# The decayed queries of groups 1 to 9 on VectorE instead of GpSimd, and a reordered last wide step

## The chip, the cores and the metric

The kernel runs on one core of a Trainium2 chip. A core has five engines that run their own instruction queues side by side: TensorE (PE in the profile; its weight loads are PEld), VectorE (DVE), ScalarE (ACT), GpSimd (POOL) and SyncE (SP), which here issues nearly all DMA transfers. SBUF is the working memory, PSUM holds TensorE's results in banks of 128 x 512 fp32. The metric is the device time of one execution in microseconds.

## The reference

Two blocks follow each other. The first is linear attention with a decay `lam` per head, over 4 sequences of 768 positions with 8 heads of 64; the second picks 128 of the 768 positions of each sequence by a gate and sends them through a two-layer expert.

```python
# attention, block of 64 positions, per head
intra = ((qb @ kb.T) * lam ** (i - j) [i >= j]) @ vb
inter = (qb * lam ** (i + 1)) @ kv_state
out   = intra + inter
kv_state = lam ** 64 * kv_state + (kb * lam ** (63 - j)).T @ vb

# mixture of depths, x = out as (4, 768, 512)
scores = x @ w_gate                          # (4, 768)
top    = the 128 positions with the largest score, per sequence
y      = x; y[top] += sigmoid(scores[top]) * (relu(x[top] @ w1) @ w2)
```

## The kernel before

The work runs in 24 groups of 128 positions (6 per sequence), numbered `g`. The order on every engine is the order in which the program is written; semaphores only hold an instruction until its inputs are there or its buffer is free. The main loop is software-pipelined: step `g` finishes group `g` and starts group `g + 1`.

Groups 0 to 8 are "wide" (`WIDE = 9`): their masked scores are taken over the whole 128 positions. Groups from 9 on are "narrow": two blocks of 64. Step 8 is the last wide step, and it prepares group 9, the first narrow one. From step 8 on, the steps also carry pieces of the expert of an earlier sequence.

The names, as the profile prints them:

- `kn`, `qn`, `vn`: keys, queries and values of a group, loaded by SyncE; `w_sb`: one of 16 pieces (256 KB each) of the expert's weights, eight of w1 (line 103) and then eight of w2 (line 108), loaded by SyncE between the groups. In what place of that queue each stands is set by `WEIGHTS_WITH`: so many pieces behind `kn` (or `qn`) of that group.
- `qT`, `kT`: the transposes. TensorE writes them to a PSUM bank (line 238; in the wide steps `Q_BANK` for the queries, printed as `m`), ScalarE copies them to SBUF (line 242).
- `qs`: the queries times their decay `qpow` (lines 250 and 252), read from `qT` and needed by TensorE in `from_states` (line 357). `kd`: the decayed keys (line 222). `decayed`: the state times its decay (line 327). All three are GpSimd's before.
- `su`: the scores in PSUM; `p`: masked scores (VectorE, line 282 wide, 288 narrow); `o`: the output in PSUM, made from `p` and `vn` (line 369 wide, 377 narrow) and from `state` and `qs` (line 357); `x_b`: the output copied to SBUF (ScalarE, line 399); `state`: the next state (VectorE, line 346).
- `xg`, `sc`: the product with `w_gate` and its sum, the gate score of each position (VectorE, line 419); `sc_row`: these scores as a row (TensorE line 439, ScalarE line 442); `table`: the comparison of a group's scores with those of all earlier positions of its sequence (VectorE, line 449, growing from 128 to 768 columns), whose columns TensorE sums (line 464).
- `xs`: the chosen rows, fetched by an indirect DMA of GpSimd (line 519); TensorE transposes them (line 532, the piece `gate`), ScalarE copies them to `xsT`, and eight pieces `hidden(f)` follow (line 569, 8 matmul instructions each in the trace): `hidden(0)` to `hidden(3)` read the first four pieces of w1, `hidden(4)` to `hidden(7)` the other four, in the order in which they are loaded.

`PIECES` says how many expert pieces a narrow step runs at its three places; in step 9 these lie ahead of `row(8)` (line 439), behind it, and at the step's end.

Step 8 ends on VectorE with `next_state(19)`, then the gate score of group 8, and then `compare(7)`. What waits for the comparison and the score is the start of step 9 on TensorE: `column_sums(7)`, `row(8)`, then `from_scores(9)`.

Of the kernel before, what the change touches and what calls it, by code (L numbers as in the profile page):

```python
# [12 lines left out]
ALU = mybir.AluOpType  # L13
# [4 lines left out]
def kernel(  # L18
# [12 lines left out]
    nc = tc.nc  # L31
# [5 lines left out]
    L = 128  # L37
# [5 lines left out]
    NGR = (CAP + 127) // 128  # L43
# [5 lines left out]
    LINE = 256  # L49
    WIDE = 9  # L50
    WEIGHTS_WITH = {
        "kn": {11: 1, 12: 2, 13: 1, 14: 1, 15: 1, 16: 1},
        "qn": {8: 1, 9: 1, 10: 1, 11: 1, 12: 2, 13: 1, 14: 1, 15: 1}, "vn": {},
    }
    STORES_WITH = {
        "kn": {6: (0,), 7: (1,), 8: (2, 3), 9: (4, 5)}, "qn": {},
        "vn": {11: (6,), 12: (7,), 13: (8,), 14: (9, 10), 15: (11,), 20: (12, 13), 21: (14, 15)},
    }
    PIECES = {9: (0, 1, 3), 13: (1, 0, 1), 14: (1, 0, 1), 15: (1, 0, 2), 20: (1, 0, 1), 21: (1, 0, 1),
              22: (1, 0, 1), 23: (1, 0, 0)}  # L60
    TINY = 2.0 ** -125
    BELOW = TINY * (1.0 - 2.0 ** -24)
# [43 lines left out]
    def w2_load(f):  # L106
# [22 lines left out]
        out=lead[:, (NT - 1) * L :], in_=lead[:, (NT - 1) * L :], compare_op=ALU.is_ge,  # L129
# [84 lines left out]
    def wide(g):  # L214
        return g < WIDE
# [29 lines left out]
    def queries_decayed(g):  # L245
        if g >= NG or (wide(g) and g % NT == 0):
            return
        qs = att.tile([128, NHP, L], FP32, name="qs")
        if wide(g):
            nc.gpsimd.tensor_tensor(out=qs[:], in0=qTs[g], in1=qpow[:], op=ALU.mult)  # L250
        else:
            nc.gpsimd.tensor_tensor(  # L252
                out=qs[:].rearrange("p a (c i) -> p a c i", c=2),
                in0=qTs[g].rearrange("p a (c i) -> p a c i", c=2),
                in1=qpow[:, :, :C].unsqueeze(2).broadcast_to([128, NHP, 2, C]), op=ALU.mult,
            )
        qss[g] = qs
# [158 lines left out]
    def gate_scores(g):  # L416
        b, t = divmod(g, NT)
        xg = mod.tile([128, HD], FP32, name="xg")
        nc.vector.tensor_tensor_reduce(  # L419
            out=xg[:], in0=x_bs[b][:, t].rearrange("p a b e -> p (a b e)"), in1=wg_b[:],  # L420
            scale=1.0, scalar=0.0, op0=ALU.mult, op1=ALU.add, accum_out=scs[b][:, t : t + 1],
        )
# [264 lines left out]
    for g in range(-1, NG):  # L687
        loads_to(g + ahead(g))
        if g < 0:
            keys_decayed(0)  # L690
            transposes(0, "kT")
            transposes(0, "qT")
            scores(0)
            transposes(1, "kT")
            masked(0)
        else:
            transposes(g + 1, "qT")
            if NGR and wide(g):
                row(g - 1)
            if g > 0:  # L700
                transposes(g + 1, "kT")
            if g == 1:
                next_state(2)
        if wide(g):
            if g >= 0:
                state_products(g + 1)
            queries_decayed(g + 1)
            if g == 1:
                decay_state(4)
            if NGR and wide(g + 1) and not ends(g - 2):  # L710
                compare(g - 1)
            if g > 0:
                next_state(2 * g + 2)
            if g >= 0:
                from_scores(g)
                outputs(g)
                if g == 0:
                    nc.scalar.copy(
                        out=decay_w[:], in_=qpow[:, :, L - 1 : L].broadcast_to([128, NHP, D])
                    )  # L720
                    keys_decayed(2)
                    decay_state(2)
                if g not in kept:
                    store(g)
            else:
                state_products(0)
                next_state(0)
                query_powers()
                nc.vector.stream_shuffle(wg_b[:], wg_b[:], first)
            if not wide(g + 1):  # L730
                decay_state(2 * g + 3)
            if g == 2:
                slot_casts()
            if g in (3, 4):
                narrow_mask(g - 3)
            if g == 5:
                narrow_powers()
            if g >= 0:
                if wide(g + 1):
                    gate_scores(g)  # L740
                scores(g + 1)
            if NGR and ends(g - 2):
                from_states(g + 1)
                take((g - 2) // NT)
            if NGR and wide(g + 1):
                column_sums(g - 1)
            if g >= 0:
                masked(g + 1)
            if NGR and ends(g - 2):
                two_to_tok((g - 2) // NT)  # L750
                compare(g - 1)
            if NGR and wide(g + 1) and ends(g - 1):
                find((g - 1) // NT)
            keys_decayed(g + 2)
            if not wide(g + 1):
                next_state(2 * g + 3)
                gate_scores(g)
            elif g + 1 in qss or (g + 1) % NT == 0:
                from_states(g + 1)
            if g > 0:  # L760
                decay_state(2 * g + 4)
            if NGR and ends(g - 2):
                get((g - 2) // NT)
            if NGR and not wide(g + 1):
                compare(g - 1)
                for i in range(NGR):
                    pieces.extend(expert(0, i))
            continue
        now = PIECES.get(g, (1, 1, 1))
        from_states(g)  # L770
        settle(g)
        queries_decayed(g + 1)
        if NGR and ends(g - 3) and g - 3 < 2 * NT:
            get((g - 3) // NT)
        state_products(g + 1)
        next_state(2 * g + 2)
        decay_state(2 * g + 3)
        if NGR:
            column_sums(g - 2)
        if g - 4 >= NT and ends(g - 4) and g - 4 < 2 * NT:  # L780
            for i in range(NGR):
                pieces.extend(expert((g - 4) // NT, i))
        products(now[0])
        if NGR:
            if ends(g - 2) and g - 2 >= 2 * NT:
                take((g - 2) // NT)
                get((g - 2) // NT)
            row(g - 1)
        products(now[1])
        from_scores(g)  # L790
        outputs(g)
        if g not in kept:
            store(g)
        scores(g + 1)
        if NGR:
            compare(g - 1)
        next_state(2 * g + 3)
        masked(g + 1)
        gate_scores(g)
        flush(later)  # L800
        keys_decayed(g + 2)
        decay_state(2 * g + 4)
        products(now[2])
        if NGR and ends(g - 1):
            column_sums(g - 1)
            find((g - 1) // NT)
        if NGR and ends(g - 2) and g - 2 < 2 * NT:
            take((g - 2) // NT)
        if g - 3 >= 2 * NT and ends(g - 3):
            for i in range(NGR):  # L810
                pieces.extend(expert((g - 3) // NT, i))
            products(1)
        flush()
# [57 lines left out]
```

## Time and profile before

| | |
|---|---|
| device time, median of 3 runs | 174.32 us (174.17 to 175.76) |
| the profiled execution, its own time | 174.1 us |
| span of its trace (first to last instruction) | 172.3 us |
| TensorE busy | 159.1 us (92%) |
| VectorE busy | 103.6 us (60%) |
| GpSimd busy | 93.5 us (54%) |
| ScalarE busy | 71.0 us (41%) |
| mean granted clock of TensorE | 0.998 |

The profile is of one execution. Its span leaves out 1.8 us ahead of the first and behind the last instruction, and its own time is 0.2 us under the median. Busy shares are averages over stages that have different limits: a wide stage to about 48 us, narrow steps with expert pieces in between to about 145 us, and the last sequence's expert alone. A timeline row gives the start in microseconds from the start of the span, the length, the engine, the line and the operation; in square brackets stands how long the engine was idle before it and what released it.

### The profile page before, as it was taken

What the parts mean: (1) busy time and instruction counts of PE and PEld (TensorE: products, weight loads), DVE (VectorE), ACT (ScalarE), POOL (GpSimd) and SP (SyncE); (2) the same over time, 40 slices, a digit from 0 to 9 for tenths busy, and PEclk for the clock granted to TensorE, in tenths of its full rate; (3) what the DMA queues carried; (4) which work ended last, traced back from release to release, by engine and by line L of the source; (5) the groups of instructions that cost most, each with busy time, mean ns of one, the idle gap of its engine ahead of it and who ended that gap; (6) DMA issues with size and microseconds to landing.
All of it is one profiled execution on the core that took longest, in us unless ns stands there. A gap on an engine that the chain in (4) does not pass through costs nothing.

```text
span 172.3 us, 7863 instructions
## 1 busy us (share of the span) xinstructions
PE 159.1 (92%) x3436; PEld 131.2 (76%) x3436; DVE 103.6 (60%) x233; ACT 71.0 (41%) x191; POOL 93.5 (54%) x100
## 2 busy tenths in 40 slices
PE   7799999999877979999989999999999999989990
PEld 7689788889666969757757999866777988469970
DVE  3987899898678424766545974575575755240011
ACT  2334655544344435533535554632554544013100
POOL 6369965568796315467687636558658600220022
PEclk9999999999999999999999999999999999999999
DMA  5999899999999999999999899997411111011000
GB/s 132 232 248 225 184 246 269 254 244 287 246 237 249 259 274 269 257 316 256 237 215 232 184 216 287 286 253 196 126 65 65 65 65 61 10 50 65 0 30 30
DMA packets 81345, 31.96 MB, mean 186 GB/s; under 512 B 75676, under 2 KB 75676, under 8 KB 81312
## 3 DMA queue, kind: packets, MB, share of 16 engines
q1 hardware_dynamic: 80640, 29.37, 67.6%
q0 software_dynamic: 656, 2.10, 3.9%
q8 instruction: 27, 0.44, 1.0%
q14 instruction: 6, 0.05, 0.1%
q10 hardware_dynamic: 16, 0.01, 0.0%
HBM read 24.13 MB, written 7.34 MB: 183 GB/s over the span
## 4 chain that ended last, share of the span: by engine, by line
PE 68%; DVE 10%; DMA 6%; issue 6%; POOL 3%; SPq 2%; ACT 2%; POOLq 1%; DVEq 0%; ACTq 0%
PE m L569 16%; PE m L581 13%; PE m L238 8%; PE o L357 6%; PE o L377 5%; PE su L314 5%; PE su L272 4%; DMA w_sb<-in_moe_w_dram 3%; PE o L369 2%; DVE xg L419 2%; PE m L606 2%; DVE p L282 2%; DMA lam_b<-in_lam_dram 2%; DVE mask_w L174 2%; PE m L305 1%
## 5 line engine op out<-in xcount | busy, mean ns | idle before, releaser
L569 PE MATMUL m<-xsT,w_sb 128*128 128x128 f32 x256 | 33.9, 282 | 1.8 <-DMA w_sb<-in_moe_w_dram 1.2
L449 DVE SCALAR_TENSOR_TENSOR table<-sc_row,sc,lead 128x128 bf16<-128x128 f32 (+5 forms) x24 | 26.3, 1097 | 12.9 <-ACT sc_row L442 12.8
L569 PEld LDWEIGHTS m<-xsT,w_sb 128*128 128x128 f32 x256 | 30.5, 192 | 2.9 <-DMA w_sb<-in_moe_w_dram 1.4
L252 POOL TENSOR_TENSOR qs<-qT,qpow 128x512 f32<-128x512 f32 x15 | 20.4, 1362 | 18.1 <-ACT qT L242 16.9
L419 DVE CUSTOM_DVE_ANT_0 xg<-x_b,wg_b 128x512 f32<-128x512 f32 x24 | 24.2, 1009 | 3.1 <-ACT x_b L399 2.5
L327 POOL TENSOR_TENSOR decayed<-state,decay 128x256 f32<-128x256 f32 x25 | 18.9, 756 | 11.7 <-DVE state L346 10.8
L581 PE MATMUL m<-w_sb,hs 128*128 128x512 f32 x48 | 25.0, 623 | 0.0
L242 ACT COPY qT<-m 128x512 f32<-128x512 f32 x24 | 14.1, 587 | 20.4 <-PE m L238 18.2
L346 DVE TENSOR_TENSOR state<-su,decayed 128x256 f32<-128x256 f32 x25 | 10.6, 422 | 18.0 <-PE su L314 9.4
L573 ACT ACTIVATE hs<-m 128x128 f32<-128x128 f32 x32 | 8.9, 278 | 24.3 <-PE m L569 24.3
L222 POOL TENSOR_TENSOR kd<-kn,kpow 128x512 f32<-128x512 f32 x15 | 16.5, 1100 | 0.0
L242 ACT COPY kT<-m 128x512 f32<-128x512 f32 x24 | 14.3, 594 | 3.3 <-PE m L238 3.2
L357 PE MATMUL o<-state,qs 64*64 64x64 f32 x672 | 15.3, 224 | 0.0
L238 PE MATMUL m<-ident,qn 128*128 128x128 f32 x96 | 15.0, 279 | 0.0
L238 PE MATMUL m<-ident,kn 128*128 128x128 f32 x96 | 14.5, 273 | 0.0
L357 PEld LDWEIGHTS o<-state,qs 64*64 64x64 f32 x672 | 12.3, 134 | 2.7 <-issue 2.2
L250 POOL TENSOR_TENSOR qs<-qT,qpow 128x512 f32<-128x512 f32 x7 | 9.7, 1384 | 7.6 <-ACT qT L242 5.9
L222 POOL TENSOR_TENSOR kd<-kn,kpow_w 128x512 f32<-128x512 f32 x9 | 11.9, 1328 | 3.5 <-DVE kpow_w L179 3.5
L377 PEld LDWEIGHTS o<-vn,p 64*64 64x64 f32 x480 | 8.7, 134 | 5.7 <-issue 2.8
L288 DVE TENSOR_TENSOR p<-su,mask 128x512 f32<-128x512 f32 x15 | 10.2, 683 | 4.0 <-PE su L272 4.0
L238 PEld LDWEIGHTS m<-ident,qn 128*128 128x128 f32 x96 | 10.7, 141 | 2.1 <-issue 1.6
L272 PE MATMUL su<-qT,kT 64*64 64x64 f32 x480 | 10.7, 220 | 1.0 <-issue 0.9
(87 smaller groups left out, 249.0 us busy)
## 6 DMA issues: line engine op xcount, KB each, us to landing
kn<-in_k_dram SPq DMA_DIRECT2D x24, 256.0 KB, 4.9
qn<-in_q_dram SPq DMA_DIRECT2D x24, 256.0 KB, 4.6
vn<-in_v_dram SPq DMA_DIRECT2D x24, 256.0 KB, 4.9
out_dram<-x_b SPq DMA_DIRECT2D x24, 256.0 KB, 3.5
w_sb<-in_moe_w_dram SPq DMA_DIRECT2D x16, 256.0 KB, 5.4
xs<-out_dram,tok POOLq DMA_INDIRECT x4, 4.2
out_dram<-y,tok POOLq DMA_INDIRECT x3, 2.9
out_dram<-y_half,half_at POOLq DMA_INDIRECT x2, 2.4
```

The costliest lines, as they stand in the source:

```text
L222: nc.gpsimd.tensor_tensor(out=kd[:], in0=loaded[g][0][:], in1=pw[:].rearrange("p a b -> p (a b)").unsqueeze(2).broadcast_to([128, H, D]), ...
L238: nc.tensor.transpose(tp[:, hp * L : (hp + 1) * L], in_=t[:, 2 * hp : 2 * hp + 2, :], identity=ident[:])
L242: nc.scalar.copy(out=dst[:].rearrange("p a i -> p (a i)"), in_=tp[:])
L252: nc.gpsimd.tensor_tensor(out=qs[:].rearrange("p a (c i) -> p a c i", c=2), in0=qTs[g].rearrange("p a (c i) -> p a c i", c=2), in1=qpow[:, ...
L272: nc.tensor.matmul(su[half[c], hh, hp * C : (hp + 1) * C], lhsT=kT[half[hh], hp, half[c]], rhs=qT[half[hh], hp, half[c]], start=True, stop ...
L327: nc.gpsimd.tensor_tensor(out=t[:], in0=states[n][:], in1=(decay_w if wide(g) else decay)[:], op=ALU.mult)
L357: nc.tensor.matmul(o_[half[c if wide(g) else hh ^ c], hh, hp * D : (hp + 1) * D], lhsT=qs[half[hh], hp, half[c]], rhs=states[n][half[hh], ...
L377: nc.tensor.matmul(o_[half[hh ^ c], hh, hp * D : (hp + 1) * D], lhsT=p[half[c], hh, hp * C : (hp + 1) * C], rhs=vn[half[c], 2 * hp + hh, : ...
L419: nc.vector.tensor_tensor_reduce(out=xg[:], in0=x_bs[b][:, t].rearrange("p a b e -> p (a b e)"), in1=wg_b[:], scale=1.0, scalar=0.0, op0=A ...
L449: nc.vector.scalar_tensor_tensor(out=table[:, : (t + 1) * L], in0=rows_[b][:, : (t + 1) * L], scalar=scs[b][:, t : t + 1], in1=lead[:, (NT ...
L569: nc.tensor.matmul(ph, lhsT=w1_sb[:, dc, f * 128 : (f + 1) * 128], rhs=keep["xsT"][:, dc, :], start=(dc == 0), stop=(dc == NDC - 1),)
L581: nc.tensor.matmul(py[:], lhsT=keep["hs"][:, f, :], rhs=w2_sb[:, f, :], start=(f == 0), stop=(f == NFC - 1),)
```

## The change

Four edits. Line numbers of the changed kernel are five higher from `queries_decayed` on.

1. `queries_decayed` for groups 1 to 5, 7 and 8 (wide; groups 0 and 6 start a sequence and have none) and for group 9 is issued to VectorE and reads the transposes from `Q_BANK` in PSUM instead of their copy `qT` in SBUF. The 14 later groups stay on GpSimd as before. The copy by ScalarE stays; scores still read it.
2. In step 8, `compare(7)` stands ahead of `gate_scores(8)`.
3. `PIECES[9]`: the expert's `gate` piece of step 9 stands ahead of `row(8)` instead of behind it.
4. `WEIGHTS_WITH`: `kn` of group 11 is followed by two weight pieces instead of one, `qn` of group 12 by one instead of two.

```diff
     WEIGHTS_WITH = {
-        "kn": {11: 1, 12: 2, 13: 1, 14: 1, 15: 1, 16: 1},
-        "qn": {8: 1, 9: 1, 10: 1, 11: 1, 12: 2, 13: 1, 14: 1, 15: 1}, "vn": {},
+        "kn": {11: 2, 12: 2, 13: 1, 14: 1, 15: 1, 16: 1},
+        "qn": {g: 1 for g in range(8, 16)}, "vn": {},
     }
...
-    PIECES = {9: (0, 1, 3), 13: (1, 0, 1), 14: (1, 0, 1), 15: (1, 0, 2), 20: (1, 0, 1), 21: (1, 0, 1),
+    PIECES = {9: (1, 0, 3), 13: (1, 0, 1), 14: (1, 0, 1), 15: (1, 0, 2), 20: (1, 0, 1), 21: (1, 0, 1),
...
         if wide(g):
-            nc.gpsimd.tensor_tensor(out=qs[:], in0=qTs[g], in1=qpow[:], op=ALU.mult)
+            nc.vector.tensor_tensor(
+                out=qs[:].rearrange("p a i -> p (a i)"), in0=Q_BANK[:],
+                in1=qpow[:].rearrange("p a i -> p (a i)"), op=ALU.mult,
+            )
         else:
-            nc.gpsimd.tensor_tensor(
+            eng = nc.vector if wide(g - 1) else nc.gpsimd
+            src = Q_BANK[:].rearrange("p (a i) -> p a i", i=L) if wide(g - 1) else qTs[g]
+            eng.tensor_tensor(
                 out=qs[:].rearrange("p a (c i) -> p a c i", c=2),
-                in0=qTs[g].rearrange("p a (c i) -> p a c i", c=2),
+                in0=src.rearrange("p a (c i) -> p a c i", c=2),
                 in1=qpow[:, :, :C].unsqueeze(2).broadcast_to([128, NHP, 2, C]), op=ALU.mult,
             )
...
             if not wide(g + 1):
                 next_state(2 * g + 3)
+                if NGR:
+                    compare(g - 1)
                 gate_scores(g)
...
             if NGR and not wide(g + 1):
-                compare(g - 1)
                 for i in range(NGR):
                     pieces.extend(expert(0, i))
```

VectorE in wide step 4 before, from the masked scores of group 4 to those of group 5:

```order
L282 TENSOR_TENSOR p<-su,mask_w 128x1024
L449 SCALAR_TENSOR_TENSOR table,ranks<-sc_row,sc,lead 128x512
L419 ISA xg,sc<-x_b,wg_b 128x512
L419 ISA sc 128x1
L468 TENSOR_TENSOR ranks<-ranks,m_128 128x3
L282 TENSOR_TENSOR p<-su,mask_w 128x1024
```

The same stretch of VectorE's queue now (`m_126` is `Q_BANK`):

```order
L287 TENSOR_TENSOR p<-su,mask_w 128x1024
L250 TENSOR_TENSOR qs<-m_126,qpow 128x512
L454 SCALAR_TENSOR_TENSOR table,ranks<-sc_row,sc,lead 128x512
L424 ISA xg,sc<-x_b,wg_b 128x512
L424 ISA sc 128x1
L473 TENSOR_TENSOR ranks<-ranks,m_128 128x3
L287 TENSOR_TENSOR p<-su,mask_w 128x1024
```

One product came in between the masked scores and the comparison; it waits for ScalarE's copy out of the same bank, not for TensorE alone. The same row left GpSimd's queue.

VectorE at the end of step 8 and the start of step 9 before:

```order
L288 TENSOR_TENSOR p<-su,mask 128x2x256
L346 TENSOR_TENSOR state<-su,decayed 128x256
L419 ISA xg,sc<-x_b,wg_b 128x512
L419 ISA sc 128x1
L449 SCALAR_TENSOR_TENSOR table,ranks<-sc_row,sc,lead 128x256
L346 TENSOR_TENSOR state<-su,decayed 128x256
```

And now:

```order
L293 TENSOR_TENSOR p<-su,mask 128x2x256
L351 TENSOR_TENSOR state<-su,decayed 128x256
L454 SCALAR_TENSOR_TENSOR table,ranks<-sc_row,sc,lead 128x256
L424 ISA xg,sc<-x_b,wg_b 128x512
L424 ISA sc 128x1
L351 TENSOR_TENSOR state<-su,decayed 128x256
```

The comparison and the gate score changed places; nothing else moved there.

SyncE's queue before, from the keys of group 11 to the first pieces of w2:

```order
L81 DMA kn<-in_k_dram 128x8x64
L103 DMA w_sb<-in_moe_w_dram 128x512
L81 DMA qn<-in_q_dram 128x8x64
L103 DMA w_sb<-in_moe_w_dram 128x512
L81 DMA vn<-in_v_dram 128x8x64
L411 DMA out_dram<-x_b 128x512
L81 DMA kn<-in_k_dram 128x8x64
L103 DMA w_sb<-in_moe_w_dram 128x512 x2
L81 DMA qn<-in_q_dram 128x8x64
L103 DMA w_sb<-in_moe_w_dram 128x512
L108 DMA w_sb<-in_moe_w_dram 128x512
```

And now:

```order
L81 DMA kn<-in_k_dram 128x8x64
L103 DMA w_sb<-in_moe_w_dram 128x512 x2
L81 DMA qn<-in_q_dram 128x8x64
L103 DMA w_sb<-in_moe_w_dram 128x512
L81 DMA vn<-in_v_dram 128x8x64
L416 DMA out_dram<-x_b 128x512
L81 DMA kn<-in_k_dram 128x8x64
L103 DMA w_sb<-in_moe_w_dram 128x512 x2
L81 DMA qn<-in_q_dram 128x8x64
L108 DMA w_sb<-in_moe_w_dram 128x512
```

The eight pieces of w1 were the 4th behind `kn` of group 11, the 5th behind `qn` of 11, the 6th and 7th behind `kn` of 12 and the 8th behind `qn` of 12. Now the 4th and 5th stand behind `kn` of 11, the 6th behind `qn` of 11, the 7th and 8th behind `kn` of 12: the 8th passes one load of queries, and `qn` and `vn` of group 11, a store, and `kn` and `qn` of group 12 stand one place later.

## Rows read from the trace of the kernel before

**Rows 1.** Chain of waits, 40 to 66 us: start us, length us, what.

```profile
52.84 0.18 PE m L464
...
56.98 5.60 DMA w_sb<-in_moe_w_dram
...
62.63 0.49 PE m L569 x2
```

**Rows 2.** Busy time per window: engines, PEclk, DMA share, GB/s.

```profile
50.00:62.60 12.60, 9.28 (x212) 8.49 (x203) 7.69 (x18) 4.83 (x15) 6.86 (x7) 1.00 0.95 251
62.60:100.00 37.40, 36.34 (x885) 28.68 (x886) 22.84 (x52) 18.06 (x52) 23.60 (x24) 1.00 0.97 248
```

**Rows 3.** Timeline of one wide step, all engines: start us, length us, what.

```profile
26.27 1.21 DVE L282 TENSOR_TENSOR p<-su,mask_w 128x1024 f32<-128x1024 f32 x1
...
26.94 0.59 ACT L242 COPY qT<-m 128x512 f32<-128x512 f32 x1 [1.32 <-PE m L238]
...
27.61 1.28 POOL L250 TENSOR_TENSOR qs<-qT,qpow 128x512 f32<-128x512 f32 x1 [1.88 <-ACT qT L242]
27.73 1.71 DVE L449 SCALAR_TENSOR_TENSOR table<-sc_row,sc,lead 128x512 bf16<-128x512 f32 x1 [0.25 <-ACT sc_row L442]
...
28.74 0.59 ACT L399 COPY x_b<-o 128x512 f32<-128x512 f32 x1 [0.55 <-PE o L369]
28.84 2.94 POOL L222 TENSOR_TENSOR kd<-kn,kpow_w 128x512 f32<-128x512 f32 x2
...
29.37 1.52 DVE L419 CUSTOM_DVE_ANT_0 xg<-x_b,wg_b 128x512 f32<-128x512 f32 x1
...
30.89 1.21 DVE L282 TENSOR_TENSOR p<-su,mask_w 128x1024 f32<-128x1024 f32 x1
```

**Rows 4.** Instructions of VectorE by line: count, busy us, mean ns, idle before.

```profile
L288 DVE TENSOR_TENSOR p<-su,mask 128x512 f32<-128x512 f32 x15 | 10.2, 683 | 4.0 <-PE su L272 4.0
```

**Rows 5.** Timeline of VectorE where GpSimd is idle or just ending.

```profile
33.97 0.69 DVE L419 CUSTOM_DVE_ANT_0 xg<-x_b,wg_b 128x512 f32<-128x512 f32 x1 [0.73 <-ACT x_b L399]
...
34.66 1.22 DVE L282 TENSOR_TENSOR p<-su,mask_w 128x1024 f32<-128x1024 f32 x1
...
61.19 0.75 DVE L449 SCALAR_TENSOR_TENSOR table<-sc_row,sc,lead 128x512 bf16<-128x512 f32 x1 [1.04 <-ACT sc_row L442]
```

**Rows 6.** Timeline at the end of the last wide step, 49 to 53 us.

```profile
49.53 2.85 DVE L419 CUSTOM_DVE_ANT_0 xg<-x_b,wg_b 128x512 f32<-128x512 f32 x1
...
49.88 0.72 POOL L327 TENSOR_TENSOR decayed<-state,decay 128x256 f32<-128x256 f32 x1
...
50.57 1.25 POOL L252 TENSOR_TENSOR qs<-qT,qpow 128x512 f32<-128x512 f32 x1
```

**Rows 7.** Timeline of TensorE, 49 to 63 us.

```profile
50.00 0.66 PE L314 MATMUL su<-vn,kd 64*64 64x64 f32 x32
...
54.64 2.94 PE L569 MATMUL m<-xsT,w_sb 128*128 128x128 f32 x24
57.42 0.60 PE L238 MATMUL m<-ident,qn 128*128 128x128 f32 x4
...
60.63 0.83 PE L569 MATMUL m<-xsT,w_sb 128*128 128x128 f32 x6
```

**Rows 8.** The fourth weight load alone, by tile: duration ns, start us; landing.

```profile
L103 SPq DMA_DIRECT2D w_sb<-in_moe_w_dram x1: 1287/1287/1287, 47.2 to 47.2; - x1
...
DMA to landing us min/median/max: 6.8/6.8/6.8
```

**Rows 9.** The load of the queries of group 11, by tile: duration, start; landing.

```profile
L81 SPq DMA_DIRECT2D qn<-in_q_dram x1: 586/586/586, 48.5 to 48.5; - x1
...
DMA to landing us min/median/max: 6.2/6.2/6.2
```

**Rows 10.** Timeline of SyncE, 53 to 58 us: start us, length us, what.

```profile
56.04 0.90 SPq L81 DMA_DIRECT2D qn<-in_q_dram  x1
```

**Rows 11.** All weight loads, by tile: time to landing.

```profile
DMA to landing us min/median/max: 4.4/5.4/6.8
```

## The prediction

> **What bounds the kernel now.** I read the chain of waits first. From about 62.6 us to the end it is nearly all TensorE; [rows 2] say the same: 36.34 of 37.40 us busy from 62.6 to 100. So whatever the change gives must be there at 62.63 us, when the last two products of `hidden(4)` start; later on TensorE works a fixed list, and a shift at 62.63 reaches the end almost whole. What ended last there is not an engine: the chain shows 5.60 us of a weight load issued at 56.98, landed at 62.58 [rows 1]. It is the eighth piece of w1. TensorE had done the six products before it from 60.63 to 61.46 and then stood for 1.2 us [rows 7].
>
> Why does that load come so late? SyncE's queue holds it behind keys, queries, other pieces and a store, and the DMA engines are full: a share of 0.95 and 251 GB/s from 50 to 62.6, 0.97 and 248 GB/s after [rows 2]. Those transfers have their data and buffers long before; a faster attention step does not bring them forward. So there are two clocks up to 62.6 us: that of the engines, and that of the weight loads.
>
> On the clock of the engines two things are lost. In step 9 TensorE ends `state_products(10)` at 50.66 and goes on at 52.84 [rows 1, 7]: 2.18 us, waiting for `table`, which VectorE has behind a gate score of 2.85 us, 49.53 to 52.38 [rows 6]. And each wide step is longer than it must be: step 4 takes 4.62 us from `p` to `p` (26.27 to 30.89), of which `table` has 1.71 and `xg` 1.52 [rows 3], where the same instructions need 0.75 and 0.69 when GpSimd is not in the way [rows 5]. The rows show why. GpSimd's `qs` runs from 27.61 to 28.89, and `table`, begun at 27.73, ends half a microsecond after that; `xg`, from 29.37 to 30.89, runs beside two `kd` that together last to 31.78 [rows 3]. The gate score of 2.85 us lies beside `decayed` and `qs`, which last to 51.82, and ends 0.56 later [rows 6]. `p`, which has one input in PSUM and one in SBUF, takes 1.21 us beside a busy GpSimd and an idle one alike [rows 3, 5].
>
> **The change part by part.** *The product on VectorE.* Eight instructions leave GpSimd, 1.28 us each [rows 3], some 10 us; eight come to VectorE. The trace has no such product there; the nearest row is the narrow `p`, with the same 512 elements and one PSUM input: 0.683 us [rows 4]. The bounds are the 1.21 of the wide `p` with 1024 elements above, and half of 0.683 below; I take 0.69, that is 5.5 us on VectorE (2.7 to 9.7). The wait that it adds is for ScalarE's copy: in step 4 that ended at 27.53 and `p` at 27.48 [rows 3], so 0.05 us. Behind it stand the comparison, the state, the gate score and the next `p`.
>
> What it gives back lies in `table`: with GpSimd's `qs` gone from beside it, 1.71 becomes 0.75. So step 4 would be 1.21 + 0.69 + 0.75 = 2.65 us to the gate score, which then waits for `x_b`, ready at 29.33, that is 3.06 after `p` began [rows 3]; 3.06 + 0.69 + 0.1 for the small ones = 3.85 if the gate score is not held, 3.85 + 1.0 if one `kd` still stands before it (4.85). Step 5, whose gate score ran in 0.69, did take 3.77, from 30.89 to 34.66 [rows 3, 5]. So a step goes from 4.62 to something between 3.85 and 4.85. Over the eight steps that is between 6 us less and 2 us more; I take 2 us less at the end of step 8, the middle.
>
> The Trainium skill (SBUF — State Buffer, section "Who interferes with whom") says that a VectorE instruction with two SBUF inputs and a GpSimd instruction that reads SBUF exclude each other for a whole instruction, and that VectorE with at most one SBUF input is not held. By that rule the moved product runs free, as the constant 1.21 us of `p` leads one to expect, and `table` regains all of its 0.96 us; but the gate score stays as it is, since both its inputs are in SBUF.
>
> *The comparison ahead of the gate score, and `gate` ahead of `row(8)`.* TensorE's `column_sums(7)` then waits for a comparison of 256 columns, less than the 0.75 us of 512 [rows 5], and no longer for the 2.85 us in front of it. `row(8)` still waits for the gate score, but four expert transposes now stand before it; four such take 0.60 us with the tail of the last [rows 7], of which I count 0.4. GpSimd has one `qs` less in front, so its later work also comes 1.28 us earlier. Of the 2.18 us TensorE regains at least those 0.4, at most all; add the wide steps, and TensorE is ready for `hidden(0)` 0.4 to 4 us earlier than 54.64 [rows 7].
>
> It cannot use the most of that. `hidden(0)` needs the fourth piece of w1, issued at 47.2 and landed 6.8 us later, at 54.0 [rows 8], and its place in SyncE's queue is unchanged. Three quarters of `hidden(0)` can run before, so the group of 24 products (2.94 us, 54.64 to 57.42 with the next transposes [rows 7]) ends at best 1.2 us earlier, about 56.2. The last products of `hidden(4)` are then ready to start between 61.46 - 1.2 = 60.3 and 61.46 - 0.4 = 61.0.
>
> *The weight pieces.* The eighth piece passes one load of queries. In the trace that load was issued at 56.04 and the piece at 56.98 [rows 1, 10]; so it is issued 0.94 us earlier and, with the same 5.6 us, lands at 61.64. All weight loads took 4.4 to 6.8 us [rows 11]: 60.4 to 62.8. That lies behind the 60.3 to 61.0 of TensorE, so the load still sets the time: 62.58 becomes 61.64, a gain of 0.94. If the load came quicker, TensorE caps the gain at 62.63 - 60.3 = 2.3.
>
> The loads that now stand one place later: the queries of group 11 landed at 48.5 + 6.2 = 54.7 [rows 9], with 0.94 more 55.7; their transposes start at 57.42 [rows 7], then at 56.2. The cover is 0.5 us; if it goes, it costs what is missing, and below the load of the eighth piece that is hidden again. The other moved loads are needed after these.
>
> Sum, against the profiled execution: 174.1 - 0.94 = 173.2 us; the median of the runs is 0.2 higher, so **173.4 us**.
>
> **The rivals.**
>
> *All of TensorE's gain counts.* If the eighth piece lands near its quickest (60.4), or the DMA stream itself comes forward, TensorE's own readiness decides: -1.6 to -2.3, so 172.4 with 172.0 as its end. For it: landing times spread by 2.4 us. Against: the DMA share of 0.95, and a landing of 5.6, just above their median of 5.4 [rows 2, 11].
>
> *No change that can be seen.* Where pieces that are issued close together share the engines, passing one load need not bring the eighth piece in earlier; it lands at 62.3 to 62.6 and all else waits for it. 174.2. For it: the fourth piece took 6.8 us and a load before it less [rows 8, 11]. Against: SyncE issues at the pace at which transfers end, and what is ahead in the queue is 256 KB less.
>
> *Slower: the gate score loses to GpSimd in each wide step.* The state releases `decayed` on GpSimd and stands just ahead of the gate score on VectorE; `decayed` (0.72) starts first, and `kd` follows at once, now that no `qs` lies between (1.2 us: half of 2.94 less the 0.56 of the gate score that ran between two of them [rows 3, 6]). Such a case is in the trace: `xg` did not get in between `decayed` and `qs` [rows 6]. Then a step of the kind of step 4, with a state (0.4, a little over half of the 0.683 for half the elements), takes 1.21 + 0.69 + 0.75 + 0.4 + 0.72 + 1.2 + 0.6 = 5.57 us against 4.62. By the program `decayed` follows in steps 1, 2, 5, 6 and 7: five times 0.95 = 4.75 us later, in the other steps nothing gained. Less the 0.4, `hidden(4)` is ready at 61.46 + 4.35 = 65.8 instead of 62.63: +3.2, so 177.5. It costs anything only from +0.6 us on in the wide steps (61.46 - 0.4 + 0.6 = 61.66, the landing of the eighth piece). The exclusion rule of the Trainium skill (same page, same section) would be the mechanism of this rival; it does not say who comes first when both wait. Against it: in step 4 `xg` did come in between two `kd`, which together took 2.94 us [rows 3].
>
> **How the numbers follow.** The forecast (the eighth piece's landing sets the time, 173.4, own range 172.7 to 173.9): 0.52. No change, 174.2: 0.2. TensorE's gain in full, 172.4 (172.0 to 172.6): 0.18. Slower, 177.5 (174.8 to 178): 0.1. The range 172.2 to 174.7 leaves out nearly all of the last and about half of the third, together 0.19. Within 1% of 174.32, which is about what a measurement tells from no change here, means 172.58 to 176.06. Faster by more: most of the third case and a little of the first, 0.18. Slower by more: 0.07. Same: 0.75.
>
> **What would show it.** In the profile after: line 250 on VectorE seven times and line 257 once, at about 0.69 us; `table` in the wide steps near 0.75 us for 512 columns; no wait of about 2 us of TensorE for `table`; TensorE at `hidden(0)` waiting for a weight load at about 54; and again a wait of `hidden(4)` for a weight load, which ends at about 61.6. Wrong would be: that wait gone with the chain going through engines instead (then a rival with another sign holds, as the wide steps went), or gate scores of 2 us and more in the wide steps. I am also wrong if something after 62.6 us, which I took as fixed, gives way or comes up.

## The result and the profile after

| | before | after |
|---|---|---|
| device time, median (runs) | 174.93 us (21) | 173.18 us (21) |
| range of the runs | 172.46 to 178.03 us | 170.3 to 176.2 us |
| ratio, with its 95% interval | | 0.9871 (0.983 to 0.9912) |
| the profiled execution: own time, span | 174.1, 172.3 us | 173.85, 172.1 us |
| TensorE busy in the span | 159.1 us | 160.0 us |

The 173.18 us lies 0.2 us from the 173.4 forecast. The change itself came out larger than forecast: the forecast went from 174.3 to 173.4 us, 0.5%; the medians differ by 1.75 us, 1.0%, and the ratio says 1.3%. The ratio compares only the runs within 1.5% of the fastest run of each kernel, 7 of the 21 of after, so it need not agree with the medians, and the profiled execution of after (173.85 us) is not among the 7. The runs of one kernel spread over nearly 6 us here, so a single trace is one draw from that spread. The execution profiled of after ends only 0.2 us ahead of the one of before, and its parts are worth more than its end.

The wide step first. VectorE in step 4 of after, and at the end of step 8 (start, length, line, operation, and in brackets the idle time before it):

```profile
26.69 1.21 DVE L287 TENSOR_TENSOR p<-su,mask_w 128x1024 f32<-128x1024 f32 x1
28.03 0.69 DVE L250 TENSOR_TENSOR qs<-m,qpow 128x512 f32<-128x512 f32 x1
28.64 0.74 DVE L454 SCALAR_TENSOR_TENSOR table<-sc_row,sc,lead 128x512 bf16<-128x512 f32 x1
29.77 1.42 DVE L424 CUSTOM_DVE_ANT_0 xg<-x_b,wg_b 128x512 f32<-128x512 f32 x1 [0.38 <-ACT x_b L404]
31.20 1.21 DVE L287 TENSOR_TENSOR p<-su,mask_w 128x1024 f32<-128x1024 f32 x1
...
48.86 0.48 DVE L454 SCALAR_TENSOR_TENSOR table<-sc_row,sc,lead 128x256 bf16<-128x256 f32 x1
...
49.26 1.21 DVE L424 CUSTOM_DVE_ANT_0 xg<-x_b,wg_b 128x512 f32<-128x512 f32 x1
```

The product is there at 0.69 us, `table` fell from 1.71 to 0.74 [rows 3], and the gate score of step 8 from 2.85 to 1.21 us [rows 6]. `xg` of step 4 still meets one `kd` (29.61 to 30.65, below). GpSimd in the same step:

```profile
25.10 1.04 POOL L222 TENSOR_TENSOR kd<-kn,kpow_w 128x512 f32<-128x512 f32 x1 [2.25 <-DMA kn<-in_k_dram]
29.61 1.04 POOL L222 TENSOR_TENSOR kd<-kn,kpow_w 128x512 f32<-128x512 f32 x1 [3.46 <-DMA kn<-in_k_dram]
```

The brackets are new. GpSimd now waits for keys, 6.2 us in three places from 12 to 52 us; in the trace of before it never did there. Next the place that the forecast rests on, TensorE in steps 9 and 10 of after:

```profile
50.67 0.69 PE L319 MATMUL su<-vn,kd 64*64 64x64 f32 x32 [1.15 <-DMA vn<-in_v_dram]
51.30 0.18 PE L469 MATMUL m<-ones,table 128*128 128x1 bf16 x1
51.33 0.63 PE L537 MATMUL m<-ident,xs 128*128 128x128 f32 x4
...
53.10 2.94 PE L574 MATMUL m<-xsT,w_sb 128*128 128x128 f32 x24
...
59.09 1.25 PE L574 MATMUL m<-xsT,w_sb 128*128 128x128 f32 x8
60.27 0.69 PE L382 MATMUL o<-vn,p 64*64 64x64 f32 x32
```

The wait of 2.18 us for `table` is gone (51.30 has no bracket), one of 1.15 us for values has come, and the eight products of `hidden(4)` run from 59.09 with no wait for a weight load that this view prints (it prints idle times above 0.15 us; a shorter one is found below). The windows of [rows 2], now of after (busy time and count of PE, PEld, DVE, ACT and POOL, then granted clock, DMA share, GB/s):

```profile
50.00:62.60 12.60, 11.93 (x276) 11.12 (x277) 6.99 (x18) 5.96 (x19) 6.38 (x6) 1.00 1.06 277
62.60:100.00 37.40, 35.08 (x819) 27.01 (x819) 23.35 (x52) 16.47 (x47) 24.19 (x24) 1.00 0.96 237
```

TensorE is busy for 11.93 us of the first window instead of 9.28. The product of `p` and `vn` of group 10 (line 382, before 377) starts at 60.27; in the trace of before it was this:

```profile
62.63 0.49 PE L569 MATMUL m<-xsT,w_sb 128*128 128x128 f32 x2 [1.16 <-DMA w_sb<-in_moe_w_dram]
63.05 0.69 PE L377 MATMUL o<-vn,p 64*64 64x64 f32 x32
...
137.33 0.69 PE L377 MATMUL o<-vn,p 64*64 64x64 f32 x32
```

So 2.78 us are won there. They do not last. In the second window TensorE has 35.08 us busy against 36.34. Two of the rows in which after stands still, and the same product of group 22:

```profile
82.74 0.21 PE L497 MATMUL m<-place,hit 128*128 128x2 bf16 x3 [1.47 <-issue]
...
87.94 0.46 PE L277 MATMUL su<-qT,kT 64*64 64x64 f32 x15 [0.66 <-issue]
...
137.11 0.69 PE L382 MATMUL o<-vn,p 64*64 64x64 f32 x32
```

Of 2.78 us at group 10 only 137.33 - 137.11 = 0.22 is left at group 22. Matched product by product, 2.5 of the 2.56 us that went lie, on balance, at 13 single products, 1.6 of them at the one at 82.74. The first of these rows is the second half of a group of six products on the same inputs: nothing that the profile names was missing.

Last, SyncE's queue after:

```profile
51.39 1.31 SPq L416 DMA_DIRECT2D out_dram<-x_b  x1
52.79 0.39 SPq L81 DMA_DIRECT2D kn<-in_k_dram  x1
53.23 2.11 SPq L103 DMA_DIRECT2D w_sb<-in_moe_w_dram  x2
55.39 1.22 SPq L81 DMA_DIRECT2D qn<-in_q_dram  x1
```

And the eighth piece alone (length of its issue in ns, its start in us, then the us to its landing), and the seventh product of `hidden(4)`, the first of the two that need this piece:

```profile
L103 SPq DMA_DIRECT2D w_sb<-in_moe_w_dram x1: 420/420/420, 54.9 to 54.9; - x1
...
DMA to landing us min/median/max: 4.9/4.9/4.9
...
59.85 0.38 PE L574 MATMUL m<-xsT,w_sb 128*128 128x128 f32 x1
```

The piece is the second of the two from 53.23 on. Its issue starts at 54.92 instead of 56.98 [rows 1], 2.06 us earlier and not 0.94, and it lands 4.88 us later, at 59.80 instead of 62.58. The first six products of `hidden(4)` start 0.11 us apart; the seventh starts 0.20 us behind the sixth, 0.05 us after that landing, as it did in the trace of before (62.63 after 62.58). So the wait for the load is still there in this execution, 0.09 us long, and the 2.78 us won at group 10 are the 2.78 us by which the load landed earlier.

Part of this is that SyncE's queue itself had come forward. Just ahead of the keys of group 12 it was held by a store, for 1.31 us in after and for longer in before:

```profile
50.69 3.25 SPq L411 DMA_DIRECT2D out_dram<-x_b  x1
```

What held that store is not shown. The profile puts 2.8 us of it down to ScalarE's `sc_row` of step 9, but the rows that it stores (group 6) had been copied at 37.79. Nor is it shown that the change brought the queue forward: in the six traces with the old place of the piece (before, e2, e3, e4, e10, e11) its issue starts anywhere from 54.9 to 58.5 us, in the six with the new place (after, e1, e5, e6, e7, e9) from 54.9 to 57.8.

### The profile page after: what moved, and what is told of

The parts are those of the page before. It is cut to its first block, busy times and chain, and to the rows that moved or that the text cites. A ratio compares the mean times of both kernels' runs of the same rounds, so it can differ in the third digit from the quotient of the medians.

```text
span 172.1 us, 7861 instructions
## 1 busy us (share of the span) xinstructions
PE 160.0 (93%) x3436; PEld 132.2 (77%) x3436; DVE 103.8 (60%) x241; ACT 70.6 (41%) x191; POOL 81.9 (48%) x92
## 4 chain that ended last, share of the span: by engine, by line
PE 87%; DMA 5%; issue 3%; ACT 1%; POOLq 1%; DVE 1%; POOL 0%
PE m L574 18%; PE m L586 13%; PE m L238 12%; PE o L362 8%; PE o L382 6%; PE su L270 5%; PE su L277 5%; PE o L374 5%; PE su L319 4%; DMA vn<-in_v_dram 4%; PE m L310 3%; PE m L168 2%; PE m L611 2%; PE m L469 2%; PE m L444 2%
## 5 line engine op out<-in xcount | busy, mean ns | idle before, releaser
L454 DVE SCALAR_TENSOR_TENSOR table<-sc_row,sc,lead 128x128 bf16<-128x128 f32 (+5 forms) x24 | 24.3, 1011 | 12.9 <-ACT sc_row L447 12.9
L257 POOL TENSOR_TENSOR qs<-qT,qpow 128x512 f32<-128x512 f32 x14 | 19.8, 1413 | 16.8 <-ACT qT L242 14.3
L424 DVE CUSTOM_DVE_ANT_0 xg<-x_b,wg_b 128x512 f32<-128x512 f32 x24 | 20.1, 839 | 3.1 <-ACT x_b L404 2.3
L222 POOL TENSOR_TENSOR kd<-kn,kpow_w 128x512 f32<-128x512 f32 x9 | 10.4, 1155 | 10.1 <-DMA kn<-in_k_dram 6.5
L319 PE MATMUL su<-vn,kd 64*64 64x64 f32 x432 | 10.8, 220 | 1.3 <-DMA vn<-in_v_dram 1.2
```

The costliest lines, as they stand in the source:

```text
L222: nc.gpsimd.tensor_tensor(out=kd[:], in0=loaded[g][0][:], in1=pw[:].rearrange("p a b -> p (a b)").unsqueeze(2).broadcast_to([128, H, D]), ...
L257: eng.tensor_tensor(out=qs[:].rearrange("p a (c i) -> p a c i", c=2), in0=src.rearrange("p a (c i) -> p a c i", c=2), in1=qpow[:, :, :C].u ...
L424: nc.vector.tensor_tensor_reduce(out=xg[:], in0=x_bs[b][:, t].rearrange("p a b e -> p (a b e)"), in1=wg_b[:], scale=1.0, scalar=0.0, op0=A ...
L454: nc.vector.scalar_tensor_tensor(out=table[:, : (t + 1) * L], in0=rows_[b][:, : (t + 1) * L], scalar=scs[b][:, t : t + 1], in1=lead[:, (NT ...
```

## The experiments

The theory after the result: the eighth piece's landing sets step 10, and the change gains by moving it. The rival: TensorE's and GpSimd's work sets it, and the product on VectorE is what gains. A third came up on the way: whichever wait is taken away, another transfer is late next.

Twelve kernels were measured in three sets, each on one chip with runs of the kernel before beside it: 30 with e1 to e4 (median 174.29 us), 11 with e5 to e8 (174.01), 35 with e9 to e12 (173.92).

**e1: the weight pieces alone (edit 4).**

```diff
-        "kn": {11: 1, 12: 2, 13: 1, 14: 1, 15: 1, 16: 1},
+        "kn": {11: 2, 12: 2, 13: 1, 14: 1, 15: 1, 16: 1},
```

(with the line of `qn` as in the change)

> The kernel before with the weight order alone (the eighth piece of w1 passes one load of queries). If the landing of that piece alone sets step 10 (the step on which the forecast rests), nearly all of the whole change's gain is here: 0.9 to 1.2 us less, ratio about 0.994, and the profile has no wait of hidden(4), or a shorter one. If TensorE's own readiness sets step 10, TensorE still stands 2.2 us for the comparison in step 9 and the gain is 0 to 0.5 us, ratio 0.997 to 1.000.

**e2: the product alone (edit 1).**

```diff
-            nc.gpsimd.tensor_tensor(out=qs[:], in0=qTs[g], in1=qpow[:], op=ALU.mult)
+            nc.vector.tensor_tensor(
+                out=qs[:].rearrange("p a i -> p (a i)"), in0=Q_BANK[:],
...
```

> The kernel before with the decayed queries of groups 1 to 9 on VectorE alone. If the load sets step 10: no change, 0.998 to 1.002. If TensorE's readiness does: the wide steps become 1 to 2 us shorter in sum and GpSimd is freer at the end of step 8, so 1 to 1.5 us less, ratio 0.992. The rival of the slower wide steps: gate scores of 2 us and more in steps with a state, 1 us or more slower. The comparisons in the wide steps fall to their undisturbed lengths (0.75 us at 512 columns) in any case.

**e3: the order alone (edits 2 and 3).**

```diff
-    PIECES = {9: (0, 1, 3),
+    PIECES = {9: (1, 0, 3),
...
+                if NGR:
+                    compare(g - 1)
                 gate_scores(g)
...
-                compare(g - 1)
```

> The kernel before with the comparison ahead of the gate score in step 8 and the expert's transposes ahead of row(8) in step 9. The load theory: no change, 0.998 to 1.002, with a longer wait of TensorE for the weights. The readiness theory: the 2.2 us wait for the comparison shrinks by 0.4 to 2.2 us, and 0.5 to 1.2 us of it reach the end, ratio 0.993 to 0.997.

**e4: after, with the weight pieces as before (edits 1, 2, 3).**

```diff
-        "kn": {11: 2, 12: 2, 13: 1, 14: 1, 15: 1, 16: 1},
+        "kn": {11: 1, 12: 2, 13: 1, 14: 1, 15: 1, 16: 1},
```

(with the line of `qn` as before)

> The changed kernel with the weight order of before. The load theory: nothing is left of the gain, 0.998 to 1.002 against before, and hidden(4) waits 1.5 us or more for the eighth piece. The readiness theory: nearly all is left, about 0.988, and hidden(4) does not wait or waits under 0.5 us.

**e5: after, with the product on GpSimd (edits 2, 3, 4).**

```diff
-            nc.vector.tensor_tensor(
-                out=qs[:].rearrange("p a i -> p (a i)"), in0=Q_BANK[:],
...
+            nc.gpsimd.tensor_tensor(out=qs[:], in0=qTs[g], in1=qpow[:], op=ALU.mult)
...
```

> The changed kernel with all decayed queries on GpSimd again (order of step 8 and 9 and weight order stay changed). If GpSimd's relief is what counts: no more than 0.5 us of the gain is left, ratio 0.996 to 1.000. If the order in steps 8 and 9 and the weights carry it: 0.988 to 0.992.

**e6: after, with the old order (edits 1, 4).**

```diff
-    PIECES = {9: (1, 0, 3),
+    PIECES = {9: (0, 1, 3),
...
-                if NGR:
-                    compare(g - 1)
                 gate_scores(g)
...
+                compare(g - 1)
```

> The changed kernel with the old order in steps 8 and 9. If relief of GpSimd counts by itself: 0.988 to 0.992. If product and order are only worth something together (the gain of the wide steps is waited away in step 9 behind the gate score): 0.996 to 1.000, with TensorE waiting 1 us or more for the comparison or the gate score in step 9.

**e7: after, and GpSimd forms the same products again, into a tile that nobody reads.**

```diff
+        if wide(g - 1):
+            again = att.tile([128, NHP, L], FP32, name="again", bufs=2)
+            nc.gpsimd.tensor_tensor(out=again[:], in0=qTs[g], in1=qpow[:], op=ALU.mult)
```

> The changed kernel, and GpSimd forms the same products once more into a tile that nobody reads, at the place in its queue where they stood. If the gain is that GpSimd no longer holds VectorE's two-input instructions: the comparisons go back to 1.1 to 1.9 us and with 0.69 us more on VectorE per wide step the kernel is at or above before, ratio 0.998 to 1.015. If the gain comes from elsewhere (order, weights, products that no longer stand in GpSimd's way to TensorE): within 0.5% of the changed kernel, 0.985 to 0.992.

**e8: after, with the eighth piece of w1 four places later** (the fifth to seventh come later too).

```diff
-        "kn": {11: 2, 12: 2, 13: 1, 14: 1, 15: 1, 16: 1},
+        "kn": {11: 1, 12: 1, 13: 2, 14: 2, 15: 1, 16: 1},
```

> The changed kernel with the eighth piece of w1 four places later in SyncE's queue (three later than before). If the landing of that piece sets step 10 after the change as it did in the trace of before: about 3 to 4 us slower than the changed kernel, ratio 1.005 to 1.012 against before. If TensorE comes later than the piece by a margin of 1 us or more: 2 to 3 us slower than the changed kernel, 1.000 to 1.005. If weights do not matter at all there: 0.987.

**e9, e10, e11: no product of step 10 needs the late pieces**, in after, in before, and in e2.

```diff
+                col = f % (NFC // 2) if b == 0 else f
...
-                        ph, lhsT=w1_sb[:, dc, f * 128 : (f + 1) * 128],
+                        ph, lhsT=w1_sb[:, dc, col * 128 : (col + 1) * 128],
```

> The changed kernel, but for the first sequence's expert hidden(4) to hidden(7) read the columns of hidden(0) to hidden(3) of w1, so that no product of step 10 needs the fifth to eighth piece (the loads are still made; this part of the first sequence's expert is computed with other weights). If the landing of the eighth piece still sets step 10 after the change: faster than the changed kernel, 171 to 172 us, ratio to the kernel before 0.975 to 0.983. If TensorE's own readiness sets it after the change, as its profile shows: the same as the changed kernel, ratio 0.985 to 0.99.

> The kernel before, with the same edit (hidden(4) to hidden(7) of the first sequence's expert read the columns of hidden(0) to hidden(3)). If the landing of the eighth piece is what sets step 10 before, as the prediction has it: the 1.2 us stall of hidden(4) goes and the time falls by about 1 us, ratio 0.993 to 0.995. If another wait steps in: 1.000.

> Only the product moved to VectorE, with the same edit (hidden(4) to hidden(7) of the first sequence's expert read the columns of hidden(0) to hidden(3)). If the product alone gave no clear gain (ratio 0.996) because the eighth piece's landing held it up, this gives the whole gain: ratio 0.983 to 0.988. If the product needs the other order in step 8 for another reason than that load: 0.995 or more.

**e12: after, with the weight pieces one load earlier.**

```diff
-        "kn": {11: 2, 12: 2, 13: 1, 14: 1, 15: 1, 16: 1},
-        "qn": {g: 1 for g in range(8, 16)}, "vn": {},
+        "kn": {11: 2, 12: 1, 13: 1, 14: 1, 15: 1, 16: 1},
+        "qn": {g: 1 for g in range(7, 16)}, "vn": {},
```

> The changed kernel with the weight pieces one load earlier: the first behind the queries of group 7, the second of two behind the keys of group 12 gone, so that the eighth piece of w1 comes one place earlier, and the keys, values and queries of groups 8 to 10 one place later. If the eighth piece bounds the changed kernel: 0.5 to 1 us faster than the changed kernel, ratio to the kernel before 0.98 to 0.985. If the data of groups 8 to 10, which come just in time, bound it: 0.5 to 2 us slower than the changed kernel, ratio 0.99 to 1.0, with waits for keys or values between 36 and 52 us.

What was measured (ratio to the kernel before on the same chip):

| | edits | median us (runs) | ratio (95% interval) |
|---|---|---|---|
| e1 | 4 | 174.43 (12) | 0.9971 (0.9918 to 1.0024) |
| e2 | 1 | 174.87 (12) | 0.9963 (0.9903 to 1.0022) |
| e3 | 2, 3 | 173.22 (12) | 0.9983 (0.9948 to 1.0019) |
| e4 | 1, 2, 3 | 171.77 (6) | 0.9868 (0.9816 to 0.9921) |
| e5 | 2, 3, 4 | 173.85 (6) | 1.0034 (0.9951 to 1.0117) |
| e6 | 1, 4 | 171.6 (6) | 0.986 (0.9782 to 0.9938) |
| e7 | all, product twice | 172.36 (6) | 0.9973 (0.9901 to 1.0045) |
| e8 | all, eighth piece late | 177.05 (6) | 1.0165 (1.0061 to 1.0268) |
| e9 | all, early columns | 173.31 (12) | 0.9997 (0.9952 to 1.0043) |
| e10 | none, early columns | 173.91 (12) | 1.0001 (0.9952 to 1.0049) |
| e11 | 1, early columns | 173.46 (12) | 0.9991 (0.9946 to 1.0036) |
| e12 | all, pieces earlier | 173.43 (12) | 0.996 (0.9917 to 1.0003) |

**What follows for the load.** e1 moves the load and nothing else, and e10 does away with the wait for it altogether; neither shows the 1 us that the theory wants of it (0.994 to 0.995). e1's interval still has room for it, e10's just has not. e4 is the counterpart: it takes the moved load away from after, its trace has a wait of 1.10 us for the eighth piece again, and its ratio is 0.9868 all the same, where the theory wanted 0.998 to 1.002:

```profile
63.72 0.49 PE L574 MATMUL m<-xsT,w_sb 128*128 128x128 f32 x2 [1.10 <-DMA w_sb<-in_moe_w_dram]
```

The move does what it was made for: `hidden(4)` has no such wait in e1, e5, e6, e7 and e12, which have it, and waits in before, e2 and e4 (1.16, 1.92 and 1.10 us), which have not; e3 has no wait without it. The times of the runs do not follow that wait. In e10's trace the wait is gone and the product of `p` and `vn` of group 10 starts at 61.90 instead of 63.05, as foretold; TensorE's waits from 36 to 66 us were then others (us in total, times, longest):

```profile
PE su L314 <- DMA vn<-in_v_dram: 1.0, 1, 1.0
PE m L464 <- DVE table L449: 0.9, 1, 0.9
PE su L314 <- DVE two L500: 0.4, 1, 0.4
```

e8 shows the other side. With the eighth piece later, `hidden(4)` waits twice for loads, and the kernel is slower than before, by more than the 0.5 to 1.2% that was expected:

```profile
59.62 0.61 PE L574 MATMUL m<-xsT,w_sb 128*128 128x128 f32 x4
61.26 0.49 PE L574 MATMUL m<-xsT,w_sb 128*128 128x128 f32 x2 [1.03 <-DMA w_sb<-in_moe_w_dram]
65.06 0.79 PE L574 MATMUL m<-xsT,w_sb 128*128 128x128 f32 x2 [3.31 <-DMA w_sb<-in_moe_w_dram]
```

So the load stands at the margin: it costs when it is late by 3 us, and no run shows a clear gain where it comes earlier. e12, with the piece another place earlier, does not beat after's ratio either (0.996); in its profiled execution the queries and values of the wide steps were late, as its expectation had for that case (rows under the last heading).

**What follows for the product.** In e7 GpSimd works as before beside VectorE's product. Step 4 of e7, VectorE and then GpSimd:

```profile
28.32 1.33 DVE L457 SCALAR_TENSOR_TENSOR table<-sc_row,sc,lead 128x512 bf16<-128x512 f32 x1
```

```profile
27.83 1.29 POOL L264 TENSOR_TENSOR again<-qT,qpow 128x512 f32<-128x512 f32 x1 [1.94 <-ACT qT L242]
29.07 1.49 POOL L222 TENSOR_TENSOR kd<-kn,kpow_w 128x512 f32<-128x512 f32 x1
```

`table` is back at 1.33 us and ends 0.53 after `again`, as it ended half a microsecond after `qs` [rows 3]. That part of the mechanism is shown: `table` is long because of GpSimd's instruction beside it. The rule of the Trainium skill (SBUF — State Buffer, section "Who interferes with whom"), that a VectorE instruction with two SBUF inputs and a GpSimd instruction that reads SBUF exclude each other, agrees with 0.74 us in after and 1.33 in e7.

The time of e7 does not decide whether this relief is the gain. Its ratio (0.9973, 0.9901 to 1.0045) misses the two forecasts (0.998 to 1.015, and 0.985 to 0.992), and its interval reaches into both. By the median e7 is 1.65 us faster than before on its chip, about as much as after, although `table` is long again.

How much of it arrives is read from the masked scores `p` of groups 0 and 7. Their distance is 31.93 us before (7.38 to 39.31) and 30.89 after (7.94 to 38.83), in these rows, first of before and then of after:

```profile
7.38 1.23 DVE L282 TENSOR_TENSOR p<-su,mask_w 128x1024 f32<-128x1024 f32 x1 [0.20 <-PE su L265]
...
39.31 1.21 DVE L282 TENSOR_TENSOR p<-su,mask_w 128x1024 f32<-128x1024 f32 x1
...
7.94 1.23 DVE L287 TENSOR_TENSOR p<-su,mask_w 128x1024 f32<-128x1024 f32 x1 [0.65 <-PE su L270]
...
38.83 1.22 DVE L287 TENSOR_TENSOR p<-su,mask_w 128x1024 f32<-128x1024 f32 x1
```

Over all profiled executions it is 31.6 to 32.1, 31.9 on average, in the six that form the product on GpSimd (before, e1, e3, e5, e7, e10), and 30.1 to 32.2, 31.1 on average, in the eight that do not: 0.8 us in seven steps. In those eight GpSimd waits for keys for 6 to 15 us between 12 and 52 us; in the six, for 0.2 us at most. Two steps later little of it can be seen: from `p` of group 0 to `p` of group 9 the six take 42.1 us on average and the eight 41.9, in a spread of 39.8 to 44.2.

**What stays open** is which edit carries the gain of the whole. By the ratios of the result and of the first two sets it takes the product and one edit more: 0.9871, 0.9868 and 0.986 with it, 1.0034 without (e5), 0.9963 alone. The third set does not bear that out: e9, which is after but for the early columns, came to 0.9997, and e11, which should have had the whole gain, to 0.9991. By the medians of the same runs e9 is 0.6 us faster than before and e11 0.5. The medians also draw another picture of the rest: e3, without the product, is 1.07 us faster than before, and e9 (173.31) lies 0.13 us from after (173.18), while the kernel before, measured beside each, differs by 1.0 us (173.92 and 174.93). Six to twelve runs of kernels that spread over 2 to 8 us do not part effects of 1 us, and whether e9 lacks the gain by its edit, by its chip or by its draw cannot be told.

## Why the prediction was right, and where not

**The number** held: 173.4 against 173.18 us. That is in part luck. The forecast started from a median of 174.32 us of three runs and took 0.94 off; the 21 runs of before have 174.93, and 1.75 came off by the medians, 1.0%, and 1.3% by the ratio. So the change is about twice the forecast one, at the edge of the 1% that the forecast called the same or beyond it, and the path to it did not hold in its sizes. The rival "no change that can be seen" is out: the ratio's interval ends at 0.9912.

**The product's cost and the exclusion:** right. 0.69 us forecast, 0.683 mean over seven; `table` at 0.74 for 512 columns where 0.75 was said; gate score of step 4 still held by one `kd` (1.42 us), so 4.51 us for the step, within 3.85 to 4.85. The size at the end was too large: 2 us by the end of step 8, and 0.8 by step 7 on the averages above. A term left out is the supply of keys: once GpSimd is free, it waits for them. That these waits are what took the rest of the 2 us is not shown.

**The rival of a gate score that loses to GpSimd:** did not come. No gate score in the wide steps took over 1.42 us.

**"So the load still sets the time":** in after's execution this came true, but by 0.09 us, and the size of the term failed. The landing was to move from 62.58 to 61.64, by 0.94, and within 60.4 to 62.8; it moved to 59.80, by 2.78: the issue came 2.06 us earlier and the time from issue to landing was 0.72 us shorter. TensorE was to be ready between 60.3 and 61.0, since `hidden(0)` would wait for the fourth piece until 54.0; that piece was issued at 46.27 instead of 47.21, `hidden(0)` started at 53.10 without a wait, and TensorE was ready before 59.80. So 2.78 us came at group 10, more than the 2.3 that the rival "all of TensorE's gain counts" allowed. The step under both is that the places of the loads in time were taken from one execution and moved by one load; the issue of the eighth piece varies by 3 us and more between the traces, and why it was early in after is open. And e10 shows that taking that wait away from the kernel before gives nothing measurable: one wait in one execution is not a bound of the program.

**"Later on TensorE works a fixed list":** this failed, and in the two profiled executions it is why so little of the 2.78 us is left at the end. After's execution lost 2.56 of its 2.78 us between groups 10 and 22. The prediction named "something after 62.6 us, which I took as fixed" as a way of being wrong; what gave way are standstills of TensorE, which the last section follows. From the product of `p` and `vn` of group 10 to the end of the span the fourteen profiled executions take 107.6 (e4) to 111.8 us (after) for the same work; from that of group 22 on, all take 35.0 us.

**The 0.94 us** was therefore no right size: 2.78 us at step 10 and 0.22 at group 22 in the two executions, and 1.75 us between the medians. That 173.4 lies so near 173.18 is luck. What bounds the kernel from about 50 to 62 us may be better told as a DMA system that is full (shares of 0.95 and 1.06 in the first windows of both kernels) and has something late at each step: keys, values, a weight piece, or what the last section shows. That is a reading of the traces; no run tests it. From 62.6 to 100 us TensorE is busy for 36.34 and 35.08 of 37.40 us.

## What to carry to other kernels

Where the DMA engines are full over a whole stage, a wait at the end of the chain may name only the transfer that was late in that execution, not a bound that can be moved: test it by a kernel that does not need that transfer at all (e10) before pricing its removal. Taking an engine out of another's way may be worth only what the next supply allows, as the waits for keys here suggest; look at how early the data of the next steps land before counting the freed time. And a stretch of "fixed work" behind the change is fixed only as far as several executions agree on it. A wait too short for a view to print can still be the one that sets the time: compare the spacing of the products around it.

## What the hardware showed beyond that

**TensorE's standstills without a named cause lie at fixed instructions.** TensorE in the profiled execution of e3:

```profile
43.80 0.58 PE L357 MATMUL o<-state,qs 64*64 64x64 f32 x24 [0.68 <-issue]
...
50.39 0.34 PE L272 MATMUL su<-qT,kT 64*64 64x64 f32 x8 [2.51 <-issue]
...
55.17 0.58 PE L272 MATMUL su<-qT,kT 64*64 64x64 f32 x24 [0.62 <-issue]
```

and in that of e1:

```profile
44.58 0.58 PE L357 MATMUL o<-state,qs 64*64 64x64 f32 x24 [1.11 <-issue]
...
50.21 0.34 PE L272 MATMUL su<-qT,kT 64*64 64x64 f32 x8 [1.56 <-issue]
...
56.34 0.58 PE L272 MATMUL su<-qT,kT 64*64 64x64 f32 x24 [1.64 <-issue]
```

Both stop at the same three products, for 0.62 to 2.51 us, 3.8 us together in e3 and 4.3 in e1. From the first to the second of these stops TensorE runs 127 matmuls, to the third 126, each with a weight load; after's stops at 82.74 and 87.94 are 127 apart. The page of after has beside the data a queue of instructions:

```profile
q8 instruction: 27, 0.44, 1.1%
```

These are 27 packets of 16 KB. TensorE has 3436 matmuls and as many weight loads, 6872, or 255 for each packet, which is the distance of the stops. The trace also has the time of each packet. In e3 packets of this queue end at 42.37, 48.93 and 54.01 us, in e1 at 43.27, 49.02 and 54.97, in after at 81.46 and 86.70; TensorE goes on 1.2 to 1.5 us behind each. The packet ahead of e3's longest stop started at 47.97, when TensorE had stood since 47.88, and took 0.96 us: it was late, not slow. So each of these stops ends shortly after 16 KB of instructions have arrived, and the likely cause is that TensorE waits for them; that the queue is TensorE's own is read from the counts. That full DMA engines are why a packet starts late is not shown; no run here took the other transfers away. The Trainium skill (Runtime: NRT & Kernel Launch, section "Instruction fetch mechanics") has blocks of 16 KiB, 256 instructions, fetched by the engine's own DMA queue, which agrees with the counts, and calls the cost of crossing a block mostly hidden; in these traces stops of up to 2.51 us were not.

**Late data can cost twice.** TensorE in e12 at the end of the wide steps:

```profile
41.25 0.66 PE L238 MATMUL m<-ident,qn 128*128 128x128 f32 x4 [1.00 <-DMA qn<-in_q_dram]
...
43.56 0.87 PE L310 MATMUL m<-vn,kd 128*64 128x64 f32 x16 [1.11 <-DMA vn<-in_v_dram]
44.16 1.98 PE L374 MATMUL o<-vn,p 128*64 128x64 f32 x32
```

and the windows around it:

```profile
41.00:43.00 2.00, 1.20 (x9) 0.96 (x9) 1.40 (x3) 1.06 (x3) 0.00 (x0) 1.00 1.03 263
43.00:45.00 2.00, 1.44 (x32) 1.47 (x34) 0.68 (x2) 0.18 (x1) 0.64 (x1) 0.72 0.98 286
45.00:47.00 2.00, 2.00 (x46) 1.88 (x44) 0.21 (x1) 0.59 (x1) 1.09 (x2) 0.50 0.98 270
```

Behind the stretch from 41 to 43 us, of which TensorE worked 1.20 us, the granted clock fell to 0.50, the lower of its two levels (1.2 instead of 2.4 GHz), and 32 products that take 1.10 to 1.15 us at the full clock took 1.98. e2, e4 and e6, also with the product on VectorE, show the same after waits for queries and values at this place. The other four with the product on VectorE do not, though e9 waits 1.45 us at once for values there; nor does any of the six traces with the product on GpSimd. One late load can so lose more than the wait itself.
